# One-hot rows of two index tables stored tile by tile, and a sum of tokens with its first gather put ahead of a query product

## The chip, the cores and the metric

The kernel runs on one core of one Trainium2 chip. The metric is the device time of one execution in microseconds, lower is better. A core has a matrix engine (PE, with its weight loads listed apart as PEld), a vector engine (DVE), a scalar engine (ACT), GpSimd (POOL) and a sync engine (SP), which here issues most DMAs. Each engine works through its own instructions in order and waits on semaphores of the others.

## The reference

An attention block with sketched features feeds a mixture of experts with one expert for each token.

```python
a, b = einsum('rd,bhsd->bhsr', S1, x), einsum('rd,bhsd->bhsr', S2, x)  # phi of q and of k
phi = outer(a, b)                      # 8 x 8 = 64 features for each head and token
kv = einsum('bhsf,bhsd->bhfd', k_p, v); z = sum(k_p, axis=2)
attn = (q_p @ kv) / (q_p @ z + 1e-6)   # B=4, H=4, S=1088, D=32
x = attn.transpose(0, 2, 1, 3).reshape(4352, 128)
logits = normed(x) @ normed(expert_emb).T / tau          # 8 experts
expert_idx = argmax(logits); gate = softmax(logits)[expert_idx]
out[t] = gate[t] * (relu(x[t] @ w1[e]) @ w2[e]),  e = expert_idx[t]   # F = 1024
```

## The kernel before

The 4352 tokens are handled in two halves m = 0 and m = 1 (two batches each). A half has 17 tiles of 128 tokens (`NC`). The program has three stages that overlap. First, for each half, keys and values are summed into `kv` and `z`, and query features `qp` are made, turned and multiplied (`nd`), and `x` writes the attention rows with their router logits into `xg`. Second, a router for each half picks an expert for each token (`best`, `pick`), computes the token's place in a list sorted by expert (`place`, `take`, `split`), and a table turns places into token numbers. Third, 35 blocks of 128 sorted tokens are fetched by indirect DMA (`fetch`), turned, and run through `up` (w1, `ps_big<-xTb,wb`) and `down` (w2, `ps_acc` or `ps_ab<-w_sb,hT`) of their expert.

The table is the part that the change touches. A place is split in a block number `place_k` and a lane `place_r` (scaled so that it equals lane / 128). `mark` (lines 775 to 780) makes, for each tile t of tokens, a 128 x 128 matrix of zeros and ones, token by lane, by comparing `place_r` with `lanes`; all of them lie in one bf16 tile `row`, of which `row[:, :, t]` is tile t. `find` and `digit` (L844, L848) mark which block a token belongs to and put its token number there (`hits`). `sums` (lines 850 to 856) multiplies, on PE, `row[:, :, t]` as weights with the `hits` of tile t, and adds over the tiles in PSUM: 17 matmuls with 20 moving columns for the first table, which serves the first 10 blocks (half m = 0), and 34 with 56 columns for the second, which serves the other 25. `tokens` (L872) on DVE reduces the result to the list `dst_i` of token numbers, which POOL's gathers (`fetch`, L1043) use.

The order on each engine is written out by hand. `HEAD` and `ORDER` (lines 395 to 410) are lists of steps in program order; every step issues its instructions to whichever engines it uses, and each engine's order follows from it. The steps that matter here are, in `ORDER`: `mark 00` and `mark 01` (DVE, the 17 tiles in parts of 8 and 9), `find` (DVE), `exp0` (DVE, and on SP the load of the first w1), `qab 2 acc` (PE), `sums` (PE), `qp 1` (DVE, L458, features of query group 1), `tokens` (DVE), `z1` (DVE, L536), `trqp 1` (PE, L158, turns that group), `qp 3` (DVE), `kve` (PE), `fetch0` and `fetch 1` (POOL, blocks 0 and then 1 to 3), then `nd 1 0`, `x 1 0`, `turn 0` (PE turns block 0), `nd 1 1`, `x 1 1`, and after `up(0)` comes `nd 1 2`. The second table's steps are placed by tick and rank among the blocks (lines 711 to 716 and 1201 to 1216).

Of the kernel before, what the change touches and what calls it, by code (L numbers as in the profile page):

```python
# [12 lines left out]
BF16 = mybir.dt.bfloat16  # L13
I32 = mybir.dt.int32
U32 = mybir.dt.uint32
ALU = mybir.AluOpType
# [3 lines left out]
P = 128  # L20
# [6 lines left out]
HALF = P // 2  # L27
# [3 lines left out]
NM = B // 2  # L31
# [6 lines left out]
WIDE = SPAN + SPAN % 2  # L38
NEXT = 172
TWO_BANKS = (2, 3)  # L40
NCP = 8 + WIDE
# [24 lines left out]
def bview(t, free):  # L66

    return bass.AP(tensor=t.tensor, offset=t.offset, ap=[list(t.ap[0])] + [list(d) for d in free])
# [3 lines left out]
def kernel(  # L72
# [13 lines left out]
    nc = tc.nc  # L86
# [3 lines left out]
    consts = ctx.enter_context(tc.tile_pool(name="consts", bufs=1))  # L90
# [4 lines left out]
    def ps_small():  # L95
        return psum.tile([P, 512], F32, tag="t", bufs=2, name="ps_t")
# [57 lines left out]
    def mm(*args, **how):  # L154
        last["pe"] = nc.tensor.matmul(*args, **how)  # L155
# [62 lines left out]
    for h in range(H):  # L218
# [6 lines left out]
    top, rem, w, fits = (work.tile([2 * R, D], U32, tag=tag, bufs=2 if tag == "iota" else 1, name=name)  # L225
                         for tag, name in (("kv", "s_top"), ("iota", "s_rem"), ("parts", "s_w"), ("iota", "s_fits")))
# [39 lines left out]

    prefer = consts.tile([P, E], F32, name="prefer")
    lane = consts.tile([P, P], F32, name="lane")
    lanes = consts.tile([P, P, WIDE], BF16, name="lanes")
    digits = consts.tile([P, 2, NM * NCP], BF16, name="digits")  # L270

    before, ones = consts.tile([P, P], BF16, name="before"), consts.tile([P, P], BF16, name="ones")
# [12 lines left out]
    c_early = consts.tile([P, E + 1], F32, name="c_early")  # L285
    w_late = consts.tile([P, E], F32, name="w_late")
    place_k = consts.tile([P, NM * NCP], F32, name="place_k")
    place_r = consts.tile([P, NM * NCP], BF16, name="place_r")
    row = consts.tile([P, P, NM * NCP], BF16, name="row")

    nowhere = [consts.tile([P, 2, n], BF16, name=f"nowhere{n}") for n in (EARLY, LATE + SHARED)]

    def more_constants():
        nc.vector.memset(ones, 1.0 / P)
        nc.vector.memset(fours, 4.0 / P)
        nc.vector.memset(ones_e, 1.0)

        nc.vector.memset(less, -(P - 1) / (2.0 * P))
        nc.vector.memset(more, (QUART - 1) / (2.0 * P))

        nc.vector.memset(near, -(HALF + 1) / (2.0 * P))
        for i, rank in enumerate(RANKS):
            nc.vector.memset(order[:, i:i + 1], float(rank))
        nc.vector.memset(c_early, 0.0)
        nc.vector.memset(w_late, float(KEYS * E))
        for t in (place_k, place_r):
            nc.vector.memset(t, -1.0)
        for t, n in zip(nowhere, (EARLY, LATE)):
            nc.vector.memset(t, 0.0)
            nc.vector.memset(t[:, 0, :n], float(NOWHERE))  # L310
# [17 lines left out]
        nc.vector.tensor_scalar(last_first, lane[:, :E], -1.0, float(E - 1), op0=ALU.mult, op1=ALU.add)  # L328

    def wide_lanes():  # L330
        nc.vector.tensor_scalar_mul(lanes, bview(lane, [[1, P], [0, WIDE]]), 1.0 / P)

    def digits_of():
        tok_i = work.tile([P, 3, NM * NCP], I32, tag="iota", bufs=2, name="tok_i")
# [53 lines left out]
    acc, z_of, sums_of, ab_ps = {}, {}, {}, {}  # L388
# [15 lines left out]
nd 0 0; ld; ld; kab 3 ab; ld; x 0 0; ktr r; nd 0 1; ld; kab 2 t; kab r ab; ld; x 0 1; kb 2; trqp0r; nd 0 2; ld; kb 3; kp 1; kb r; nd 0 3; ld; x 0 2;  # L404
kv 0; ld; kp 2; x 0 3; qtr 1; kp 3; qtr 0; ld; kv 2; qab 0 t; qb 0; kp r; best 0; kv 3; qtr 3; qtr r; qp 0;
place 0; count; take 0; qtr 2; ld; kv 1; ld; kv r; trqp 0; total; split 0; qab 1 t; qab 3 ab; rest; mark 00; qb 1;
qab r ab; mark 01; find; exp0; qab 2 acc; sums; qb 2; qpT 0; qb 3; qb r; qp 1; tokens; z1; trqp 1; qp 3; kve; fetch0; fetch 1;
trqp 3; qpT 1; kz; qp 2; nd 1 0; ld; ld; qp r; others; w 1; x 1 0; qpT 3; norm 0; trqp 2; ld; turn 0; ld; nd 1 1; ld; x 1 1;
qpT 2
"""  # L410
# [317 lines left out]
    def router(m, c0, c1, g, bank):  # L728
        n = c1 - c0
        s = {}  # L730

        def best():
            mx = work.tile([P, n], F32, tag=f"mx_{n}", name="mx")
            nc.vector.reduce_max(out=mx, in_=lg[g][:, :n], axis=AX.X)
            nc.vector.tensor_sub(xg[g][:, :n, DM:DM + E], lg[g][:, :n], mx.unsqueeze(2).broadcast_to([P, n, E]))

        def pick():

            t = work.tile([P, n, E], F32, tag=f"lt_{n}", name="lt")
            mx = work.tile([P, n], F32, tag=f"mx8_{n}", name="mx8")  # L740
            nc.vector.scalar_tensor_tensor(out=t, in0=xg[g][:, :n, DM:DM + E], scalar=0.0,
                                           in1=bview(prefer, [[0, n], [1, E]]), op0=ALU.is_equal, op1=ALU.add)
            nc.vector.reduce_max(out=mx, in_=t, axis=AX.X)
            last["oh"] = nc.vector.tensor_tensor(out=oh[m, c0], in0=t, in1=mx.unsqueeze(2).broadcast_to([P, n, E]),
                                                 op=ALU.is_equal)
            with nc.allow_low_precision(reason="a count of at most SPAN is whole in bfloat16"):
                nc.vector.reduce_sum(out=total[m, c0], in_=oh[m, c0].rearrange("p j e -> p e j"), axis=AX.X)

        def place():

            hot = oh[m, c0]
            ps = s["ps"] = bank()[:, :n * E].rearrange("p (j e) -> p j e", e=E)
            mm(ps, before, hot, start=True, stop=False)
            for t in [base, less] + counts:
                mm(ps, ones, t.unsqueeze(1).broadcast_to([P, n, E]), start=False, stop=False)
            for j in range(1, n):
                mm(ps[:, j:], ones, hot[:, j - 1:j].broadcast_to([P, n - j, E]), start=False, stop=j == n - 1)
            counts.append(total[m, c0])  # L760

        def take():
            s["t"] = work.tile([P, n, E], F32, tag=f"lt_{n}", name="lt")
            nc.vector.tensor_mul(s["t"], s["ps"], oh[m, c0])

        def split():

            t0, t1 = m * NCP + c0, m * NCP + c1
            f = work.tile([P, n], F32, tag=f"mx8_{n}", name="mx8")
            nc.vector.reduce_sum(out=f, in_=s["t"], axis=AX.X)  # L770
            nc.vector.tensor_scalar(place_k[:, t0:t1], f, WHOLE, -WHOLE, op0=ALU.add, op1=ALU.add)
            nc.vector.scalar_tensor_tensor(out=place_r[:, t0:t1], in0=f, scalar=(P - 1) / (2.0 * P), in1=place_k[:, t0:t1],
                                           op0=ALU.add, op1=ALU.subtract)

        def mark(a=c0, b=c1):

            w = b - a + (b - a) % 2
            t0, t1 = m * NCP + a, m * NCP + a + w
            nc.vector.tensor_tensor(out=row[:, :, t0:t1], in0=lanes[:, :, :w],  # L779
                                    in1=bview(place_r[:, t0:t1], [[0, P], [1, w]]), op=ALU.is_equal)  # L780

        def write():
            for i in range(c0 // NK, c1 // NK):
                at = (2 * m + i) * S
                nc.sync.dma_start(rows[at:at + SK].rearrange("(p c) d -> p c d", p=P), xg[g][:, i * NK - c0:(i + 1) * NK - c0])
            if c1 == NC:
                for i in range(2):
                    at = (2 * m + i) * S + SK
                    nc.sync.dma_start(rows[at:at + HALF], xg[g][i * HALF:(i + 1) * HALF, 2 * NK - c0])
        return best, pick, place, take, split, mark, write  # L790


# [32 lines left out]
    def column(name, dt=F32, w=E):  # L825
        return consts.tile([P, w], dt, name=name)

    def table(which, m1, key):
# [3 lines left out]
        n, w = SIZES[which] + SECONDS[which], m1 * NCP  # L832
        s = {}
# [16 lines left out]
        def sums():  # L850
            s["ps"] = ps_small()[:, :2 * n]
            tiles = [m * NCP + c for m in range(m1) for c in range(NC)]
            mm(s["ps"], ones, nowhere[which].rearrange("p d n -> p (d n)"), start=True, stop=False)
            for t in tiles:
                mm(s["ps"], row[:, :, t], s["col"].rearrange("p d n w -> p w d n")[:, t].rearrange("p d n -> p (d n)"),
                                 start=False, stop=t == tiles[-1])

        def first_rows():
# [44 lines left out]
    def plan_late():  # L903


        left, upto, t = column("left"), column("upto1"), column("steps")
# [4 lines left out]
        s = {}  # L911
# [86 lines left out]
        def extra():  # L998
# [16 lines left out]
            f = column("extra_f", w=1)[0:1]  # L1015
# [4 lines left out]
            w = NM * NCP  # L1020
            hit = work.tile([P, 3, w], BF16, tag="lg0", bufs=1, name="extra_hit")
# [3 lines left out]
            ps = ps_small()[:, :2]  # L1025
            tiles = [m * NCP + c for m in range(NM) for c in range(NC)]
            mm(ps, ones, nowhere[0][:, :, 0], start=True, stop=False)
            for t in tiles:
                mm(ps, row[:, :, t], hit[:, 1:, t], start=False, stop=t == tiles[-1])
            with nc.allow_low_precision(reason="whole numbers of at most NOWHERE"):  # L1030
                nc.vector.reduce_sum(out=dst_i[2], in_=ps, axis=AX.X)
        return count, rest, shared, others, experts, number, start, extra
# [164 lines left out]
    count, rest, shared, others, experts, number, start, extra = plan_late()  # L1197
    find, high, low, sums, tokens, first_rows, halves = table(1, NM, lambda: late["key"])
# [106 lines left out]
```

## Time and profile before

| | us |
|---|---|
| runs of the kernel | 199.03, 200.95, 201.89 (median 200.95) |
| the profiled execution's own time | 199.14 |
| its span, first to last instruction | 197.2 |
| PE busy | 188.3 (95% of the span) |
| DVE busy | 87.9 (45%) |
| ACT busy | 99.1 (50%) |
| POOL busy | 107.6 (55%) |

The profile is of one execution. Its times count from the first instruction; the execution's own time is 1.94 us more than the span. A line of the timeline merges neighbouring instructions of one kind: start, time from the first one's start to the last one's end, engine, source line, operation, output <- input, and in brackets the idle time just before it with what ended it. Matmuls are pipelined, so a merged line ends about 0.2 us after the last one began. The fp32 matmuls appear as two passes each.

### The profile page before, as it was taken

The numbers are of one execution on the slowest core, as the hardware profiler recorded it, in microseconds if no ns is written. First come the engines' busy times: TensorE is split into PE (matmuls) and PEld (weight loads), VectorE is DVE, ScalarE is ACT, GpSimd is POOL, SyncE is SP. The second block draws the span as 40 slices with busy tenths as digits, with TensorE's granted clock in tenths as the row PEclk, the third lists the DMA queues.
The fourth block names the chain that finished last, engine by engine and source line by source line (L and its number), as shares of the span: only waits on it lengthen the run. The fifth ranks groups of instructions, "written<-read, shape, count | busy, mean of one in ns | idle before, by whom it ended". The sixth has DMA issues, their size and how long they took to land.

```text
span 197.2 us, 7104 instructions
## 1 busy us (share of the span) xinstructions
PE 188.3 (95%) x2667; PEld 177.8 (90%) x2667; DVE 87.9 (45%) x393; ACT 99.1 (50%) x280; POOL 107.6 (55%) x135
## 2 busy tenths in 40 slices
PE   7999899999979999999999999999999999999990
PEld 7677799788869999999999999999999999998890
DVE  6589868798378489922221221221221221222100
ACT  2675542437253456433564654654654654766430
POOL 4300054707713866565977767767767767733052
PEclk9999999999999999999999999999999999999999
DMA  5979968974799997544587686596665655540001
GB/s 139 345 203 276 237 172 221 331 232 124 201 281 330 285 338 209 188 136 149 149 263 237 158 288 201 155 281 211 161 195 182 160 200 180 150 137 12 3 20 32
DMA packets 29924, 38.32 MB, mean 194 GB/s; under 512 B 5721, under 2 KB 23394, under 8 KB 29890
## 3 DMA queue, kind: packets, MB, share of 16 engines
q1 hardware_dynamic: 27600, 33.18, 56.3%
q0 software_dynamic: 2240, 4.67, 7.6%
q8 instruction: 23, 0.38, 0.8%
q14 instruction: 11, 0.09, 0.2%
q10 hardware_dynamic: 50, 0.01, 0.0%
HBM read 33.25 MB, written 4.66 MB: 192 GB/s over the span
## 4 chain that ended last, share of the span: by engine, by line
PE 75%; DMA 12%; DVE 6%; issue 2%; ACT 2%; POOLq 1%; POOL 0%
PE ps_big L155 35%; PE ps_acc L155 14%; PE ps_ab L155 14%; DMA xs<-rows,dst_i 12%; PE ps_t L158 6%; PE ps_t L155 3%; PE ps_acc L111 1%; DVE xg L679 1%; DVE row L779 1%; PE ps_ab L158 1%; PE ps_acc L158 1%; POOLq L1300 1%; DVE qp L458 1%; PE ps_big L158 1%; ACT hT L1108 1%
## 5 line engine op out<-in xcount | busy, mean ns | idle before, releaser
L155 PE MATMUL ps_big<-xTb,wb 128*128 128x128 f32 (+2 forms) x608 | 70.6, 266 | 0.1
L155 PEld LDWEIGHTS ps_big<-xTb,wb 128*128 128x128 f32 (+1 forms) x608 | 66.7, 183 | 1.5 <-issue 0.9
L1149 POOL DMA_INDIRECT out_dram<-y,dst_i x35 | 36.4, 1041 | 42.3 <-ACT sq L1113 21.4
L1108 ACT ACTIVATE hT<-ps_big 128x1024 f32<-128x1024 f32 x35 | 35.8, 1023 | 41.3 <-issue 23.6
L1043 POOL DMA_INDIRECT xs<-rows,dst_i x35 | 36.7, 1048 | 13.0 <-issue 6.1
L155 PE MATMUL ps_acc<-w_sb,hT 128*128 (+2 forms) x288 | 35.1, 275 | 0.0
L1051 DVE COPY xTb<-ps_t 128x128 f32<-128x128 f32 x28 | 8.1, 291 | 57.3 <-issue 39.7
L155 PEld LDWEIGHTS ps_acc<-w_sb,hT 128*128 128x128 f32 (+2 forms) x288 | 33.3, 184 | 0.3 <-issue 0.2
L155 PE MATMUL ps_ab<-w_sb,hT 128*128 (+1 forms) x272 | 33.2, 275 | 0.0
L155 PEld LDWEIGHTS ps_ab<-w_sb,hT 128*128 128x128 f32 (+1 forms) x272 | 31.6, 187 | 0.1
L1114 POOL TENSOR_TENSOR norm<-norm,half_c 128x1 f32<-128x1 f32 x35 | 20.7, 595 | 5.2 <-ACT sq L1113 4.9
L1127 DVE TENSOR_SCALAR gate<-gate 128x1 f32<-128x1 f32 x35 | 5.3, 150 | 21.2 <-ACT probs L1124 19.7
L458 POOL TENSOR_TENSOR kp<-both 128x1024 f32<-128x1024 f32 (+1 forms) x4 | 7.2, 1812 | 12.5 <-ACT both L499 11.1
L155 PE MATMUL ps_big<-kz,held 128*64 128x82 f32 x256 | 10.7, 236 | 1.1 <-ACT xTb L1051 1.1
L1146 ACT ACTIVATE y<-ps_ab,gate 128x128 f32<-128x128 f32 x17 | 6.2, 367 | 10.9 <-PE ps_ab L155 7.1
L155 PEld LDWEIGHTS ps_big<-kz,held 128*64 128x64 f32 x256 | 9.5, 136 | 2.3 <-ACT hT L1108 1.3
L1113 ACT ACTIVATE sq<-xs 128x128 f32<-128x128 f32 x35 | 10.6, 302 | 1.5 <-DMA xs<-rows,dst_i 1.3
L1124 ACT ACTIVATE probs<-xs,norm 128x8 f32<-128x8 f32 x35 | 10.3, 295 | 1.3 <-DVE norm L1118 1.3
L1146 ACT ACTIVATE y<-ps_acc,gate 128x128 f32<-128x128 f32 x17 | 6.2, 366 | 9.4 <-PE ps_acc L155 7.0
L158 PE MATMUL ps_t<-ident,xs 128*128 128x128 f32 x35 | 9.8, 279 | 0.0
L425 ACT COPY qT<-ps_t 128x512 f32<-128x512 f32 (+1 forms) x10 | 5.1, 535 | 7.2 <-PE ps_t L158 7.2
L458 DVE TENSOR_TENSOR kp<-both 128x1024 f32<-128x1024 f32 (+1 forms) x6 | 6.4, 1088 | 2.9 <-ACT both L499 2.8
(254 smaller groups left out, 254.4 us busy)
## 6 DMA issues: line engine op xcount, KB each, us to landing
wb<-in_moe_w_dram SPq DMA_DIRECT2D x35, 512.0 KB
w_sb<-in_moe_w_dram SPq DMA_DIRECT2D x16, 256.0 KB
rows<-xg SPq DMA_DIRECT2D x4, 544.0 KB
q<-in_q_dram SPq DMA_DIRECT2D x6, 256.0 KB
k<-in_k_dram SPq DMA_DIRECT2D x3, 512.0 KB
held<-in_moe_w_dram SPq DMA_DIRECT2D x3, 512.0 KB
v<-in_v_dram SPq DMA_DIRECT2D x2, 512.0 KB
v<-in_v_dram SPq DMA_DIRECT2D x4, 256.0 KB
```

Source lines behind the costliest of these rows:

```text
L155: last["pe"] = nc.tensor.matmul(*args, **how)
L158: last["pe"] = nc.tensor.transpose(*args)
L458: last[tag] = engine.tensor_mul(t.rearrange("p j h (i k) -> p (j h) i k", i=R), ab[:, :, 0].unsqueeze(3).broadcast_to([P, n * H, R, R]), b ...
L1043: nc.gpsimd.indirect_dma_start(out=xs[i][:], out_offset=None, in_=rows[:2 * S if t == 0 else N + 1], in_offset=bass.IndirectOffsetOnAxis(a ...
L1051: (nc.scalar.copy if i < 2 or 4 <= i <= 8 else nc.vector.tensor_copy)(xT[i], ps[:, :P])
L1108: nc.scalar.activation(hT[i], ps, ACT.Relu)
L1113: nc.scalar.activation(sq, xs[i][:, :DM], ACT.Square, accum_out=norms[i])
L1114: nc.gpsimd.tensor_tensor(out=norms[i], in0=norms[i], in1=half_c, op=ALU.pow)
L1124: nc.scalar.activation(p, xs[i][:, DM:], ACT.Exp, scale=norms.pop(i)[:, 0:1], accum_out=gate[i])
L1127: nc.vector.tensor_scalar_add(gate[i], gate[i], PROB_EPS)
L1146: nc.scalar.activation(y, ps, ACT.Copy, scale=gate.pop(i)[:, 0:1])
L1149: d = nc.gpsimd.indirect_dma_start(out=out[:, :], out_offset=bass.IndirectOffsetOnAxis(ap=dst_i[t][:, j:j + 1], axis=0), in_=y[:], in_offs ...
```

## The change

Four edits go together. The tile `row` is stored with the tile number ahead of the lane: tile t is now `row[:, t]`, 128 neighbouring bf16 numbers, where before its 128 numbers lay 36 numbers apart. `lanes` shrinks from 128 x 10 numbers to 128. `place_r` holds every number twice, and `mark` compares two neighbouring lanes with such a pair, for 8 and 9 tiles (before 8 and 10, the odd count being padded); the memset of `place_r` that the padding called for goes. And in `ORDER`, `tokens` and `fetch0` stand ahead of `qp 1`, with `fetch 1` left where it was. The extra path at the end (L1029), which these inputs do not run, reads `row` in the new way as well.

```diff
-    lanes = consts.tile([P, P, WIDE], BF16, name="lanes")
+    lanes = consts.tile([P, P], BF16, name="lanes")
...
-    place_r = consts.tile([P, NM * NCP], BF16, name="place_r")
-    row = consts.tile([P, P, NM * NCP], BF16, name="row")
+    place_r = consts.tile([P, NM * NCP, 2], BF16, name="place_r")
+    row = consts.tile([P, NM * NCP, P], BF16, name="row")
...
-        for t in (place_k, place_r):
-            nc.vector.memset(t, -1.0)
+        nc.vector.memset(place_k, -1.0)
...
-        nc.vector.tensor_scalar_mul(lanes, bview(lane, [[1, P], [0, WIDE]]), 1.0 / P)
+        nc.vector.tensor_scalar_mul(lanes, lane, 1.0 / P)
...
-qab r ab; mark 01; find; exp0; qab 2 acc; sums; qb 2; qpT 0; qb 3; qb r; qp 1; tokens; z1; trqp 1; qp 3; kve; fetch0; fetch 1;
+qab r ab; mark 01; find; exp0; qab 2 acc; sums; qb 2; qpT 0; qb 3; qb r; tokens; fetch0; qp 1; z1; trqp 1; qp 3; kve; fetch 1;
...
-            nc.vector.scalar_tensor_tensor(out=place_r[:, t0:t1], in0=f, scalar=(P - 1) / (2.0 * P), in1=place_k[:, t0:t1],
+            nc.vector.scalar_tensor_tensor(out=place_r[:, t0:t1], in0=f.unsqueeze(2).broadcast_to([P, n, 2]),
+                                           scalar=(P - 1) / (2.0 * P),
+                                           in1=place_k[:, t0:t1].unsqueeze(2).broadcast_to([P, n, 2]),
                                            op0=ALU.add, op1=ALU.subtract)
...
-            w = b - a + (b - a) % 2
-            t0, t1 = m * NCP + a, m * NCP + a + w
-            nc.vector.tensor_tensor(out=row[:, :, t0:t1], in0=lanes[:, :, :w],
-                                    in1=bview(place_r[:, t0:t1], [[0, P], [1, w]]), op=ALU.is_equal)
+            w, t0 = b - a, m * NCP + a
+            nc.vector.tensor_tensor(out=row[:, t0:t0 + w].rearrange("p t (l d) -> p t l d", d=2),
+                                    in0=bview(lanes, [[0, w], [2, HALF], [1, 2]]),
+                                    in1=bview(place_r[:, t0:t0 + w], [[2, w], [0, HALF], [1, 2]]), op=ALU.is_equal)
...
-                mm(s["ps"], row[:, :, t], s["col"].rearrange("p d n w -> p w d n")[:, t].rearrange("p d n -> p (d n)"),
+                mm(s["ps"], row[:, t], s["col"].rearrange("p d n w -> p w d n")[:, t].rearrange("p d n -> p (d n)"),
```

On DVE, the instructions from the first table's two `mark`s on stand like this before. In brackets is the engine whose semaphore an instruction waits for; `row` is the marks' output, `hits` that of `find` and `digit`, `exp` that of `exp0`, `qp<-both` is the step `qp 1`, `dst_i` the step `tokens`, `z` the step `z1`.

```order
L779 TENSOR_TENSOR row<-lanes,place_r 128x128x8
L779 TENSOR_TENSOR row<-lanes,place_r 128x128x10
L844 TENSOR_TENSOR hits_1075<-at_1062,place_k 128x180 [waits DVE_49]
L848 TENSOR_TENSOR hits_1075<-hits_1075,digits 128x18x10 [waits DVE_49]
L848 TENSOR_TENSOR hits_1075<-hits_1075,digits 128x18x10
L818 TENSOR_REDUCE exp_f_1065<-le_1061 1x10
L819 TENSOR_SCALAR exp_210<-exp_f_1065 1x1 [waits DVE_49]
L458 TENSOR_TENSOR qp<-both 128x1024 [waits Activation_49]
L872 TENSOR_REDUCE dst_i_207<-ps_t 128x10 [waits PE_49]
L536 TENSOR_TENSOR z<-own,kv 128x256 x2
```

And like this with the change, in the same place of the same engine (source lines are one or two off, since lines were added and taken out).

```order
L779 TENSOR_TENSOR row<-lanes,place_r 128x1024
L779 TENSOR_TENSOR row<-lanes,place_r 128x1152
L845 TENSOR_TENSOR hits_1074<-at_1061,place_k 128x180 [waits DVE_49]
L849 TENSOR_TENSOR hits_1074<-hits_1074,digits 128x18x10 [waits DVE_49]
L849 TENSOR_TENSOR hits_1074<-hits_1074,digits 128x18x10
L819 TENSOR_REDUCE exp_f_1064<-le_1060 1x10
L820 TENSOR_SCALAR exp_210<-exp_f_1064 1x1 [waits DVE_49]
L873 TENSOR_REDUCE dst_i_207<-ps_t 128x10 [waits PE_49]
L457 TENSOR_TENSOR qp<-both 128x1024 [waits Activation_49]
L535 TENSOR_TENSOR z<-own,kv 128x256 x2
```

`dst_i`, which waits for PE's sums, moved ahead of `qp`, which does not; the marks' outputs became runs of 1024 and 1152 neighbouring numbers. On PE, ACT, POOL and SP every instruction stands where it stood.

The second table's marks stand on DVE between instructions of the blocks; here are the second mark and its neighbours with the change (before, the `row` line reads `128x128x10`, in the same place).

```order
L845 TENSOR_TENSOR hits_1707<-at_1608,place_k 128x1008
L849 TENSOR_TENSOR hits_1707<-hits_1707,digits 128x36x28
L779 TENSOR_TENSOR row<-lanes,place_r 128x1152
L1118 TENSOR_SCALAR norm<-norm 128x1
L1119 RECIPROCAL norm<-norm 128x1
```

Nothing moved there; only the mark's layout and its size differ.

## Rows read from the trace of the kernel before

**Rows 1.** The page's first two parts: busy time, share of the span and instructions of each engine, and the clock that PE was granted in 40 slices of the span, in tenths of full speed.

```profile
PE 188.3 (95%) x2667; PEld 177.8 (90%) x2667; DVE 87.9 (45%) x393; ACT 99.1 (50%) x280; POOL 107.6 (55%) x135
...
PEclk9999999999999999999999999999999999999999
```

**Rows 2.** Busy time by stretch of the span: start and end, length, then each engine's busy time and count, PE's granted clock, the DMA engines' busy share and GB/s.

```profile
45.10:51.80 6.70, 6.70 (x114) 5.93 (x114) 5.33 (x14) 4.14 (x12) 5.44 (x5) 1.00 0.54 145
51.80:55.70 3.90, 2.69 (x19) 2.12 (x21) 1.50 (x5) 1.51 (x3) 1.56 (x2) 1.00 1.00 286
55.70:85.70 30.00, 30.00 (x338) 29.61 (x339) 22.72 (x107) 15.76 (x53) 17.37 (x20) 1.00 0.81 256
85.70:87.80 2.10, 2.10 (x38) 2.10 (x35) 0.15 (x1) 0.37 (x1) 1.01 (x1) 1.00 0.63 215
87.80:165.70 77.90, 77.90 (x700) 77.78 (x699) 18.24 (x111) 40.97 (x125) 56.02 (x64) 1.00 0.65 196
165.70:192.40 26.70, 26.68 (x469) 24.94 (x467) 4.48 (x27) 14.46 (x36) 11.45 (x13) 1.00 0.24 75
```

**Rows 3.** Timeline of PE around the first table's sums and the step `trqp 1` behind them.

```profile
43.66 1.16 PE L155 MATMUL ps_t<-hits,row 128*128 128x20 bf16 x17
45.09 1.09 PE L158 MATMUL ps_big<-ident,qp 128*128 128x128 f32 x8 [0.27 <-DVE qp L458]
```

**Rows 4.** Timeline of DVE over the same stretch: the two marks, the end of `exp0`, `qp 1`, `tokens`, `z1`.

```profile
41.28 1.42 DVE L779 TENSOR_TENSOR row<-lanes,place_r 128x1024 bf16<-128x1024 bf16 x2
...
43.76 0.14 DVE L819 TENSOR_SCALAR exp<-exp_f 1x1 int32<-1x1 f32 x1
43.83 1.20 DVE L458 TENSOR_TENSOR qp<-both 128x1024 f32<-128x1024 f32 x1
44.97 0.16 DVE L872 TENSOR_REDUCE dst_i<-ps_t 128x10 int32<-128x20 f32 x1
45.05 0.74 DVE L536 TENSOR_TENSOR z<-own,kv 128x256 f32<-128x256 f32 x2
```

**Rows 5.** Timeline of PE and of DVE around the second table's sums.

```profile
85.72 2.22 PE L155 MATMUL ps_t<-hits,row 128*128 128x56 bf16 x34
87.78 2.03 PE L155 MATMUL ps_big<-xTb,wb 128*128 128x128 f32 x16
...
82.82 1.19 DVE L848 TENSOR_TENSOR hits<-hits,digits 128x1008 bf16<-128x1008 bf16 x1
...
87.98 0.20 DVE L872 TENSOR_REDUCE dst_i<-ps_t 128x20 int32<-128x40 f32 x1 [2.13 <-PE ps_t L155]
```

**Rows 6.** PE's weight loads of bf16, grouped by what is loaded: partitions x numbers, count, busy us, mean ns of one. `ones` and `before` are constant tiles whose 128 numbers are neighbours.

```profile
L155 PEld LDWEIGHTS <-row 128*128 128x128 bf16 x51 | 3.2, 167 | 0.0
...
L155 PEld LDWEIGHTS <-ones 128*128 128x128 bf16 x48 | 1.9, 97 | 0.7 <-issue 0.6
...
L155 PEld LDWEIGHTS <-before 128*128 128x128 bf16 x3 | 0.3, 99 | 0.0
```

**Rows 7.** Timeline of weight loads in the second half's `place` steps, whose matmuls have 72 moving columns or fewer.

```profile
64.45 0.34 PEld L155 LDWEIGHTS <-ones 128*128 128x128 bf16 x10
...
68.46 0.52 PEld L155 LDWEIGHTS <-ones 128*128 128x128 bf16 x16
```

**Rows 8.** DVE's instructions grouped by line and shape: count, busy us, mean ns of one, idle time before them.

```profile
L848 DVE TENSOR_TENSOR hits<-hits,digits 128x1008 bf16<-128x1008 bf16 x2 | 2.4, 1200 | 0.0
...
L779 DVE TENSOR_TENSOR row<-lanes,place_r 128x1280 bf16<-128x1280 bf16 x2 | 1.6, 818 | 0.0
...
L779 DVE TENSOR_TENSOR row<-lanes,place_r 128x1024 bf16<-128x1024 bf16 x2 | 1.4, 695 | 0.0
...
L848 DVE TENSOR_TENSOR hits<-hits,digits 128x180 bf16<-128x180 bf16 x2 | 0.6, 342 | 0.0
```

**Rows 9.** Timeline of POOL, ACT and PE, one after the other: block 0's gather, the first reader of its rows, and PE from its turn on (`nd 1 1` at 50.43, `up(0)` at 51.78, `nd 1 2` at 55.63, and `up(2)` at 62.65).

```profile
45.42 1.45 POOL L1043 DMA_INDIRECT xs<-rows,dst_i  x1 [5.61 <-DVE dst_i L872]
...
49.01 0.31 ACT L1113 ACTIVATE sq<-xs 128x128 f32<-128x128 f32 x1 [0.18 <-DMA xs<-rows,dst_i]
...
50.23 0.27 PE L158 MATMUL ps_t<-ident,xs 128*128 128x128 f32 x1
50.43 1.36 PE L155 MATMUL ps_big<-kz,held 128*64 128x82 f32 x32
51.78 2.63 PE L155 MATMUL ps_big<-xTb,wb 128*128 128x128 f32 x16
...
55.63 1.36 PE L155 MATMUL ps_big<-kz,held 128*64 128x82 f32 x32 [1.10 <-ACT xTb L1051]
...
62.65 1.96 PE L155 MATMUL ps_big<-xTb,wb 128*128 128x128 f32 x16
```

**Rows 10.** Timeline of DVE: `lanes` and the next long idle time behind it; then the last instruction of `x 1 0`, and the first of `x 1 1` and the last that reads the PSUM product of `nd 1 1`.

```profile
22.81 0.82 DVE L331 TENSOR_SCALAR lanes<-lane 128x1280 bf16<-128x1280 f32 x1
...
26.31 1.23 DVE L458 TENSOR_TENSOR kp<-both 128x1024 f32<-128x1024 f32 x1 [1.47 <-ACT both L499]
...
50.83 0.38 DVE L684 TENSOR_REDUCE lg<-parts 128x32 f32<-128x128 f32 x1
54.10 0.18 DVE L677 TENSOR_SCALAR rc<-ps_big 128x16 f32<-128x16 f32 x1 [2.88 <-remote]
...
55.20 0.28 DVE L683 TENSOR_TENSOR parts<-ps_big,rc 128x128 f32<-128x128 f32 x1
```

More of the change, by code (lines that the diff above doesn't have):

```diff
@@ L1028, in extra @@
             for t in tiles:
-                mm(ps, row[:, :, t], hit[:, 1:, t], start=False, stop=t == tiles[-1])
+                mm(ps, row[:, t], hit[:, 1:, t], start=False, stop=t == tiles[-1])
             with nc.allow_low_precision(reason="whole numbers of at most NOWHERE"):
```

## The prediction

> **What bounds the kernel now.** I read the page first: PE is busy for 95% of the span and its granted clock is full in all 40 slices, that is the 2.4 GHz level throughout [rows 1]. So the question for every edit is whether PE gets the time back or loses it. A busy share over the whole span hides where PE waits, so next I read the busy times by stretch. From 55.70 on PE has no idle time that matters: 30.00 of 30.00, 2.10 of 2.10, 77.90 of 77.90 and 26.68 of 26.70 us [rows 2]. Whatever is taken out of PE's work there shortens the program by as much, and nothing else does. From 45.10 to 51.80 PE is full too (6.70 of 6.70), so a delay that enters at 45.10 travels to 51.80 unchanged. Only 51.80 to 55.70 has slack, 2.69 busy of 3.90. Then the timeline, for the places that the change touches: the first table's sums, 17 matmuls from 43.66 to 44.82, and `trqp 1` behind them, for which PE waits 0.27 us until DVE's `qp 1` is done [rows 3, 4]; and the second table's 34 matmuls, which hold PE from 85.72 to 87.78 in the full stretch [rows 5].
>
> **The second table's sums, the gain.** 34 matmuls in 87.78 - 85.72 = 2.06 us are 60.6 ns each [rows 5]. With 56 moving columns they should not need that: matmuls with `ones` as weights and 72 columns or fewer follow each other at (0.34 - 0.097) / 9 = 27 and (0.52 - 0.097) / 15 = 28 ns [rows 6, 7]. The visible difference is the weight load: 167 ns in the mean for `row`, whose 128 numbers lie 36 numbers (72 bytes) apart, and 97 to 99 for tiles of the same size and type whose numbers are neighbours [rows 6]. With the change `row[:, t]` is such a tile. The bounds are no gain (60.6 stay) and 27 ns; I take 28, since in shape and type the new load is the one in those rows, and `before`, which is loaded once at a time and not again and again like `ones`, also takes 99. Gain: 34 x (60.6 - 28) = 1.11 us, all of it in a stretch where PE never waits. The marks and digits that these sums need are early enough: the last digit ends at 82.82 + 1.19 = 84.01, 1.7 us ahead of 85.72 [rows 5].
>
> The Trainium skill, "TensorE: Matmul & The Clock Gate", section on weight-path perf modes, says that the fast weight load is on for 128 weights of a type other than fp32 and reads its chunks packed or strided, within a step of some thousand elements. By that rule alone old and new load would be equally fast and the 1.11 us would not come; 167 against 97 ns in this trace says that the step does cost, and I go by the rows. What the rule would make of the time is the third rival below.
>
> **The first table's sums and the new order, the loss.** The same 32 ns on 17 matmuls end the sums 0.54 us sooner, at 44.28 instead of 44.82 [rows 3]. Before, this would have been worth nothing: PE's next work waits for `qp 1`, which DVE began at 43.83 while the sums ran [rows 4]. With the change `tokens` stands first on DVE and waits for the sums. In the second table it starts 0.04 us after the last sum ends (85.72 + 2.22 = 87.94, then 87.98) [rows 5], so here at 44.32, and the next instruction starts 0.08 later as now (44.97, 45.05) [rows 4]: `qp 1` starts at 44.40, not 43.83. PE starts `trqp 1` 1.26 us after `qp 1` starts (43.83, 45.09), so at 45.66: a delay of 0.57 us. Behind `tokens` on DVE wait `qp 1`, `z1` and the later products, moved by 0.5 us or less since `tokens` no longer stands between them; PE, moved by 0.57, does not wait for them anew.
>
> Two smaller terms come ahead of it. The marks go from 1024 and 1280 numbers to 1024 and 1152; by their own slope, (818 - 695) / 256 = 0.48 ns a number, that is 0.06 us less [rows 8]. `place_r` is written twice over, 17 numbers more at (1200 - 342) / 828 = 1.04 ns: 0.02 us more [rows 8]. Sums, `tokens` and `qp 1` start 0.04 sooner, so the delay is 0.53 us.
>
> What the order is to buy is an earlier first gather. It starts on POOL 0.45 us after `tokens` (44.97, 45.42) [rows 4, 9], so at 44.73, 0.7 us sooner. Its rows are first read at 49.01 on ACT, and PE turns the block at 50.23, in its own order and without waiting [rows 9]. Block 0's rows are thus over a microsecond early already and the gain there is nothing; the cover is PE's own queue. Gathers 1 to 3 follow sooner by as much and are not waited for either. `lanes` shrinks to a tenth (0.82 us now), but DVE then idles 1.47 us until ACT hands it `kp`'s input [rows 10]: nothing on the path. The memset that goes lies at the very start, far ahead of any of this; I cost it at nothing too.
>
> **Does the delay reach the end?** It travels to 51.80. There stands a stall whose cause the trace does not name: `up(0)` takes 2.63 us where `up(2)` takes 1.96, and `nd 1 2` waits 1.10 us [rows 9], because its PSUM bank is held by `x 1 1`, which DVE starts at 54.10 after 2.88 us of idle time put down to "remote", though `nd 1 1` was done at 51.79 [rows 9, 10]; the DMA engines are busy all through this stretch [rows 2]. If the end of that wait is tied to DVE's and PE's progress, the 0.53 passes through; if it is tied to something that the change does not move, the slack swallows it. I take the first, since the instructions on both sides of the wait move together, and keep zero as the other bound.
>
> **Sum.** -1.11 + 0.53 = -0.58 us against the profiled execution's own 199.14: 198.56. That execution is a quick one: the mean of it and the three runs shown is 200.25, 1.11 above it. For the median of the changed kernel's runs I add that 1.11: **199.7 us**.
>
> **Rivals.**
> 1. The stall swallows the delay: only the 1.11 us remain, 198.03 on the profiled basis, 199.1 in the median. For it: the wait is long and its releaser is none of the moved engines. It could also vanish altogether (0.67 + 1.10 more): 196.8, or 197.9 in the median.
> 2. The other side: the marks run at one number a cycle. The new `place_r` operand is a pair read 64 times over, a pattern that no row shows. `L848`, also bf16 on both sides, takes 342 ns for 180 numbers and 1200 for 1008 [rows 8]; at that rate the marks take 1.22 and 1.35, 2.57 us against 1.42 now [rows 4], and everything behind them, `trqp 1` too, is late by 0.57 + 0.02 + 1.15 = 1.74 us. Sum: -1.11 + 1.74 = +0.63, or 199.8 and 200.9 in the median. It decides the sign once the two marks together take 0.6 us longer than forecast. Against it: all three operands still step by one number innermost, as in the marks of now, which run at 0.48 ns a number. The second table's marks would be 1.0 us longer and fit into their 1.7.
> 3. The loads do not get faster: the sums still end at about 44.78, `tokens` starts at 44.82, `qp 1` at 44.90, and `trqp 1` is 1.07 us late with nothing gained later: 200.2, or 201.3 in the median. Against it the 97 to 99 ns of rows 6.
>
> On rival 2, the Trainium skill's "Vector Engine (DVE) Microarchitecture Reference", section on measured stream behaviour, says that a port runs at full rate only in runs of two or more neighbouring 4-byte words, and gives 1.73 instead of 1.054 ns where one source hops at every element. A pair of `place_r` is one such word; if reading it again counts as a hop, an estimate from that page is 17 x 64 x 0.68 ns = 0.74 us more for the two marks and a sum near +0.2. No row here shows such a pattern.
>
> **Chances.** Forecast as it stands 0.50; rival 1 0.20 (0.05 of it the stall gone); rival 2 0.15; rival 3 0.10; something not seen 0.05. All medians lie between 197.9 and 201.3, and the runs shown scatter by 2.9 us; the range that leaves 2 in 10 out is **197.8 to 201.6**. A measurement of this kernel can tell about 2%, 4 us, from no change, and no case comes near that: faster 0.04, same 0.93, slower 0.03.
>
> **What would show it.** Weight loads of `row` near 97 ns; 34 sums in about 1 us; marks near 0.70 and 0.76 us; `tokens` right behind the sums and PE idle 1.3 us ahead of `trqp 1`; `up` blocks from the second table on about a microsecond earlier relative to `up(0)`. Marks above 1 us, or loads that stay at 160 ns, would make the forecast wrong, and so would a different length of the stall ahead of `nd 1 2`.

## The result and the profile after

The changed kernel takes **201.09 us** in the median of 20 runs (199.18 to 204.10), the kernel before 199.38 on the same occasion (20 runs, 198.01 to 202.71); in the means it is 201.23 against 199.74. The ratio is 1.0061 with a 95% interval of 1.0035 to 1.0087: slower by 0.4 to 0.9%, where 0.3% faster was forecast. The time lies inside the forecast range; the sign does not. The ratio leaves out runs over 1.5% above the fastest of their kernel; since the cause found below makes just such runs, the experiments are also compared by the means of all their runs.

The profiled execution took 199.18 us with a span of 197.1, against 199.14 and 197.2 before. It is one of the quickest of the 20: it shows what the edits did, and not yet why the median went up. First the page, PE's busy time and granted clock [rows 1]:

```profile
span 197.1 us, 7103 instructions
PE 186.5 (95%) x2667; PEld 175.8 (89%) x2667; DVE 87.5 (44%) x392; ACT 99.0 (50%) x280; POOL 107.1 (54%) x135
PEclk9999999999999999999999999999999999999999
```

PE does 1.8 us less work (188.3 before) in a span as long as before: the work that was saved has become idle time. The weight loads of bf16 by what is loaded, and the marks on DVE (count, busy us, mean ns) [rows 6, 8], are as forecast:

```profile
L155 PEld LDWEIGHTS <-ones 128*128 128x128 bf16 x48 | 1.9, 97 | 0.4 <-issue 0.3
...
L155 PEld LDWEIGHTS <-row 128*128 128x128 bf16 x51 | 1.5, 96 | 0.0
...
L779 DVE TENSOR_TENSOR row<-lanes,place_r 128x1152 bf16<-128x1152 bf16 x2 | 1.5, 751 | 0.0
L779 DVE TENSOR_TENSOR row<-lanes,place_r 128x1024 bf16<-128x1024 bf16 x2 | 1.4, 678 | 0.0
```

Timeline of PE around the second table's sums [rows 5]: 0.97 us from their start to the next `up`, where it was 2.06.

```profile
86.07 1.04 PE L155 MATMUL ps_t<-hits,row 128*128 128x56 bf16 x34
87.04 2.02 PE L155 MATMUL ps_big<-xTb,wb 128*128 128x128 f32 x16
```

Timeline of DVE and of PE around the first table's sums [rows 3, 4]; line 873 is `tokens`, line 457 the products, the first of them `qp 1`:

```profile
43.23 0.14 DVE L820 TENSOR_SCALAR exp<-exp_f 1x1 int32<-1x1 f32 x1
43.97 0.18 DVE L873 TENSOR_REDUCE dst_i<-ps_t 128x10 int32<-128x20 f32 x1 [0.60 <-PE ps_t L155]
44.06 1.21 DVE L457 TENSOR_TENSOR qp<-both 128x1024 f32<-128x1024 f32 x1
45.20 0.75 DVE L535 TENSOR_TENSOR z<-own,kv 128x256 f32<-128x256 f32 x2
```

```profile
43.00 0.39 PE L155 MATMUL ps_acc<-Sblk,qT 128*64 128x64 f32 x5 [0.38 <-issue]
...
43.36 0.57 PE L155 MATMUL ps_t<-hits,row 128*128 128x20 bf16 x17
45.33 1.09 PE L158 MATMUL ps_big<-ident,qp 128*128 128x128 f32 x8 [1.40 <-DVE qp L457]
...
47.20 0.66 PE L158 MATMUL ps_acc<-ident,qp 128*128 128x128 f32 x4
...
49.36 1.36 PE L155 MATMUL ps_big<-kz,held 128*64 128x82 f32 x32 [1.07 <-issue]
...
51.82 1.36 PE L155 MATMUL ps_big<-kz,held 128*64 128x82 f32 x32
```

DVE is free at 43.37 and waits 0.60 us for the sums, only then come `tokens` and `qp 1`, and PE waits 1.40 us ahead of `trqp 1`, where it waited 0.27. Counted from the start of the sums, `trqp 1` begins after 45.33 - 43.36 = 1.97 us, where it was after 45.09 - 43.66 = 1.43: the change delays it by 0.54 us in place. PE stands still three times within 7 us: 0.38, 1.40 and 1.07 us. Busy time by stretch [rows 2] (PE, its weight loads, DVE, ACT, POOL, granted clock, DMA) shows what this does later:

```profile
45.10:51.80 6.70, 5.40 (x81) 4.68 (x81) 4.44 (x12) 3.07 (x7) 4.84 (x5) 1.00 0.43 118
51.80:55.70 3.90, 3.90 (x64) 3.62 (x65) 3.06 (x10) 1.75 (x4) 0.99 (x1) 1.00 0.79 191
```

The stall of 51.8 to 55.7 is gone; the 1.07 us of "issue" ahead of `nd 1 0` (the row at 49.36) are new. DVE was half a microsecond ahead of the profile before already at the end of `exp0` (43.23, 43.76), so the two executions can't be subtracted row by row here. The page of this execution shows the full clock all through; what it can't show is that most of the others did not have it. The mean granted clock of the 20 runs goes from 0.970 to 1.000, and 13 of them lie under 0.99 (of the 20 runs of the kernel before on that occasion only the times are known). That is where the theories part.

### The profile page after: what moved, and what is told of

Its sections match the earlier page's. It is cut to its first block, busy times and chain, and to the rows that moved or that the text cites. A ratio compares the mean times of both kernels' runs of the same rounds, so it can differ in the third digit from the quotient of the medians.

```text
span 197.1 us, 7103 instructions
## 1 busy us (share of the span) xinstructions
PE 186.5 (95%) x2667; PEld 175.8 (89%) x2667; DVE 87.5 (44%) x392; ACT 99.0 (50%) x280; POOL 107.1 (54%) x135
## 4 chain that ended last, share of the span: by engine, by line
PE 72%; DMA 12%; DVE 6%; issue 5%; POOL 2%; ACT 1%; POOLq 1%
PE ps_big L155 32%; PE ps_ab L155 14%; PE ps_acc L155 14%; DMA xs<-rows,dst_i 12%; PE ps_t L158 6%; PE ps_t L155 3%; PE ps_acc L111 1%; DVE xg L678 1%; PE ps_big L158 1%; POOL xs L1044 1%; POOL norm L1115 1%; DVE lg L683 1%; PE ps_ab L158 1%; PE ps_acc L158 1%; POOLq L1301 1%
## 5 line engine op out<-in xcount | busy, mean ns | idle before, releaser
L1044 POOL DMA_INDIRECT xs<-rows,dst_i x35 | 36.2, 1034 | 11.7 <-issue 6.3
```

Of the source, the lines that this page charges most:

```text
L1044: nc.gpsimd.indirect_dma_start(out=xs[i][:], out_offset=None, in_=rows[:2 * S if t == 0 else N + 1], in_offset=bass.IndirectOffsetOnAxis(a ...
```

## Experiments

**Theory A**: the longer idle time of PE ahead of `trqp 1` lowers the granted clock in many executions. **B**: the order costs its plain delay, the clock has no part. **C**: the layout itself costs. **D**, added later: it is the earlier gather, not the wait. Each run had runs of the kernel before beside it on its chip: 23 on the first chip (layout alone, order alone, nine transposes, changed kernel), 29 on the second (wait alone, order filled, nine again, four) and 29 on the third (the rest), with means of 198.31, 198.55 and 198.81 us and 2, 5 and 6 of them under a mean clock of 0.99. "Low" below is the number of runs under 0.99; differences are those of the means of all runs with 95% intervals (1.96 standard errors; for six runs that is about a quarter too narrow, which changes no conclusion). A fall of the clock is a stretch at the lower of its two levels; what one looks like is shown below.

**The layout alone**, twice:

```diff
-qab r ab; mark 01; find; exp0; qab 2 acc; sums; qb 2; qpT 0; qb 3; qb r; tokens; fetch0; qp 1; z1; trqp 1; qp 3; kve; fetch 1;
+qab r ab; mark 01; find; exp0; qab 2 acc; sums; qb 2; qpT 0; qb 3; qb r; qp 1; tokens; z1; trqp 1; qp 3; kve; fetch0; fetch 1;
```

> The new layout of the row one-hots with the old order (tokens behind qp 1, first gather behind kve). Theory A, the clock: the order's longer idle time of PE ahead of trqp 1 (1.40 us in the changed kernel, 0.27 before) makes the granted clock fall in many executions, and the layout by itself only gains; here PE waits some 0.8 us there, so the ratio to the kernel before is 0.993 to 0.998, with a mean granted clock nearer to that of the kernel before than to the changed kernel's 0.97 to 1.00. Theory B, the plain delay: the order costs its 0.5 us at qp 1 and further waits behind it, the clock has no part in it: 1.1 us gained, ratio 0.994, clocks no matter. Theory C, the layout itself costs (shorter sums leave PE idle, or the marks disturb something): ratio 1.003 or more.

> The new layout with the old order, again, for more runs. Theory A: mean time 0.6 to 1.1 us below the kernel before, granted clocks of 0.99 to 1.00 as in the kernel before. Theory B: 1.1 us below.

Measured: ratio 0.9968 (0.9933 to 1.0003), difference -0.74 +-0.76 us, low 0 of 12; then 0.9999 (0.9955 to 1.0044), -0.42 +-1.09, low 1 of 12, less of a gain than expected. Together -0.58 +-0.67. In the two profiles PE waits 0.31 and 0.57 us ahead of `trqp 1`, not 0.8. Theory C falls: the layout does not cost. That it gains is likely, that it gains its whole 1.1 us is not shown.

**The order alone**, the kernel before with the opposite edit of that line:

> The kernel before with the new order alone, old layout. Sums end at 44.82 as before, tokens and qp 1 follow, so trqp 1 is about 1.07 us late and PE waits 1.3 us ahead of it. Theory A (clock): 1.1 us of delay and granted clocks below 1 in many runs, ratio 1.008 to 1.02. Theory B (plain delay): ratio 1.003 to 1.006, granted clocks as in the kernel before. Theory C (layout costs): ratio 1.000 to 1.005, less than the changed kernel's loss.

Measured: ratio 1.0148 (1.0084 to 1.0211), +2.67 +-1.8 us, low 4 of 6. More than the delay, and with lower clocks: A, not B. Its profiled execution kept the full clock, and has the wait in it (timeline of PE; the second row is `nd 1 1`):

```profile
45.27 1.09 PE L158 MATMUL ps_big<-ident,qp 128*128 128x128 f32 x8 [1.40 <-DVE qp L458]
...
50.58 1.36 PE L155 MATMUL ps_big<-kz,held 128*64 128x82 f32 x32
```

**The changed kernel again**, on two chips:

> The changed kernel again, on the same chip as the other three, so that its runs and granted clocks stand beside theirs. All theories: ratio 1.0035 to 1.009 to the kernel before, granted clocks of 0.97 to 1.00.

> The changed kernel a third time, beside the other three. Theory A: granted clocks below 0.99 in 4 to 8 of 10 runs, mean time 0.7 to 1.8 us above the kernel before; the runs at 0.995 and more 0.3 to 0.9 us below those of the kernel before at such clocks. Theory B: no difference between the two groups of runs.

Measured: ratio 0.9964 (0.9913 to 1.0014) on the first chip and 1.0150 (1.0084 to 1.0216) on the third, where 1.0035 to 1.009 was expected: one below, one above. By the means of all runs it is +1.19 +-1.4 us with 8 of 13 low, and +1.75 +-1.1 with 4 of 6 low. On the first chip the 8 low runs take 200.8 us in the mean, the other 5 197.5, 0.7 less than the 21 runs of the kernel before that are not low (198.1), as theory A has it. On the third chip that expectation fails: the two runs that are not low take 199.7 and 200.1, against 198.2 in the mean of the 23 runs of the kernel before that are not low. On the first chip the profile caught a low run. PE's clock by slice, the timeline of PE, then PE's busy time and granted clock in stretches of 2 us:

```profile
PEclk9999969999589999999999999999999999999998
```

```profile
47.06 0.39 PE L155 MATMUL ps_acc<-Sblk,qT 128*64 128x64 f32 x5 [1.35 <-issue]
...
47.42 0.57 PE L155 MATMUL ps_t<-hits,row 128*128 128x20 bf16 x17
49.40 1.38 PE L158 MATMUL ps_big<-ident,qp 128*128 128x128 f32 x8 [1.40 <-DVE qp L457]
...
52.19 1.11 PE L158 MATMUL ps_acc<-ident,qp 128*128 128x128 f32 x4
...
57.78 0.43 PE L155 MATMUL ps_big<-kz,held 128*64 128x82 f32 x6
```

```profile
46.00:48.00 2.00, 0.93 (x23) 1.00 0.20 57
48.00:50.00 2.00, 0.60 (x6) 1.00 0.80 219
50.00:52.00 2.00, 2.00 (x27) 0.52 0.29 86
52.00:54.00 2.00, 2.00 (x14) 0.50 0.27 67
54.00:56.00 2.00, 2.00 (x29) 0.50 0.16 37
56.00:58.00 2.00, 2.00 (x23) 0.78 0.33 33
```

This is how a fall of the clock is read: PE stands still for most of 46 to 50 us, in two waits of 1.35 and 1.40; after it has gone on with `trqp 1`, the granted clock is 0.50, the 1.2 GHz level, and PE is "busy" without a gap because every matmul takes longer (four transposes 1.11 us, 0.66 in the profile after). From `trqp 1` to `nd 1 1` it takes 57.78 - 49.40 = 8.38 us; in the run of the order alone, at the full clock, 50.58 - 45.27 = 5.31. **A fall here costs 3.07 us in place.** Two more profiles below have a fall there, with 8.30 us (wait alone) and 8.42 (four transposes) for the same stretch; the profiles with the full clock and no stop inside it have 5.30 to 5.38 (5.34 before). The profile after is at the full clock too but has its 1.07 us of "issue" inside, so it takes 51.82 - 45.33 = 6.49, and against that a fall costs 1.9. The 6 in the sixth slice is a second fall (granted clock 0.54 and 0.60 in 26 to 28 and 28 to 30 us), behind a stop of 2.48 us that ends at 25.74, ahead of all that the change touches.

**The gap filled with work that nothing needs**: nine transposes of the identity into `trqp 1`'s own PSUM bank, ahead of it, twice; and four.

```diff
+    FILL = 9
...
+            for _ in range(FILL if (m, c0) == (1, 4) else 0):
+                tp(s["ps"][0][:, :P], ident, ident)
             for p in range(2):
                 for j in range(n):
```

> The changed kernel plus nine transposes of the identity, written into trqp 1's own PSUM bank just ahead of it, so that PE is busy for about 1.2 us of its 1.40 us of idle time there; nothing else moves. Theory A (clock): granted clock back to 1.0 in nearly all runs, 0.5 to 2 us less than the changed kernel, ratio to the kernel before 0.995 to 1.000. Theory B and C: same time as the changed kernel, ratio 1.004 to 1.008, clocks below 1 as often as there.

> The changed kernel with the nine filling transposes, again, for more runs. Theory A: granted clocks of 0.99 to 1.00, mean time 0.3 to 1.0 us below the kernel before (1.11 of gain less the delay of 0.5). Theory B and D: as the changed kernel, 0.5 to 2 us above.

> The changed kernel with four filling transposes instead of nine: PE still waits about 0.85 us ahead of trqp 1. Theory A, if the clock answers to the length of PE's idle time: between the changed kernel and the filled one, clocks below 0.99 in some runs but fewer than with no filling, mean time 0.5 us below to 1.0 above the kernel before. Theory B and D: as the changed kernel.

Measured with nine: -0.78 +-1.4 us, low 0 of 6 (no ratio), then ratio 0.9899 (0.9820 to 0.9979), -0.03 +-1.5, low 1 of 6, less of a gain than the 0.3 to 1.0 expected. With four: ratio 0.9973 (0.9922 to 1.0024), +1.0 +-1.35, low 3 of 12, at the upper end of what was expected. PE in the first run with nine:

```profile
43.32 0.57 PE L155 MATMUL ps_t<-hits,row 128*128 128x20 bf16 x17
43.74 1.18 PE L158 MATMUL ps_big<-ident 128*128 128x128 f32 x9
45.29 1.09 PE L158 MATMUL ps_big<-ident,qp 128*128 128x128 f32 x8 [0.37 <-DVE qp L458]
```

`trqp 1` starts at the same time (45.29, 45.33 in the profile after), PE has more to do, and low runs go from 12 of 19 to 1 of 12, with 3 of 12 in between for the half dose. B and D have no answer to this.

**The order alone, filled**: both edits above on the kernel before.

> The kernel before with the new order (old layout) and the nine filling transposes ahead of trqp 1. Theory A: granted clocks of 0.99 to 1.00 in nearly all runs, mean time 0 to 1.2 us above the kernel before, against 2.7 us above it for the new order without the filling. Theory B and D: clocks of 0.97 to 0.99 as often as with the new order alone, 2 to 3 us above.

Measured: ratio 1.0018 (0.9976 to 1.0060), +0.28 +-0.87 us, low 1 of 12, as A has it. What the order costs beyond its delay goes with the idle time.

**The wait alone**: old layout, old order, but `qp 1` is computed twice.

```diff
             s["qp"] = features(s["ab"], s["b"], n, "qp", nc.gpsimd if by_pool else nc.vector)
+            if (m, c0) == (1, 4):
+                nc.vector.tensor_mul(s["qp"].rearrange("p j h (i k) -> p (j h) i k", i=R),
+                                     s["ab"][:, :, 0].unsqueeze(3).broadcast_to([P, n * H, R, R]),
+                                     s["b"].unsqueeze(2).broadcast_to([P, n * H, R, R]))
```

> The kernel before, old layout and old order, with the product of qp 1 computed twice into the same tile. DVE gives qp 1 to PE 1.1 to 1.2 us later, and PE waits about 1.4 us ahead of trqp 1 as it does in the changed kernel; tokens and the first gather are not moved ahead. Theory A (the idle time lowers the clock): mean granted clock 0.97 to 0.99 in about half of the runs or more, mean time 1.5 to 3.5 us above the kernel before. Theory B (plain delay): 1.1 us above it, clocks as in the kernel before (0.99 to 1.00). Theory D (it is the earlier gather's traffic that disturbs, not the wait): clocks and times as in theory B, or less.

Measured: ratio 1.0094 (1.0044 to 1.0143), +2.66 +-0.94 us, low 8 of 12. Neither `tokens` nor the gather is earlier here, so D falls: a late `qp 1` is enough. The profile caught a fall (timeline of PE, the last row `nd 1 1`, then the stretches). PE waits 0.80 us for `qp 1` there and not 1.4, because a stop of 0.93 us ahead of it had already made the sums late:

```profile
45.50 0.39 PE L155 MATMUL ps_acc<-Sblk,qT 128*64 128x64 f32 x5 [0.93 <-issue]
...
47.80 1.97 PE L158 MATMUL ps_big<-ident,qp 128*128 128x128 f32 x8 [0.80 <-DVE qp L602]
...
56.10 1.36 PE L155 MATMUL ps_big<-kz,held 128*64 128x82 f32 x32
```

```profile
44.00:46.00 2.00, 1.07 (x28) 1.00 0.58 165
46.00:48.00 2.00, 1.21 (x19) 0.88 0.50 90
48.00:50.00 2.00, 2.00 (x12) 0.50 0.46 182
```

**The gap filled with work that is needed**: `z1` on DVE ahead of `tokens` or `qp 1`, `kve` on PE ahead of `trqp 1`; once with the new order of `tokens`, once with the old one.

```diff
-qab r ab; mark 01; find; exp0; qab 2 acc; sums; qb 2; qpT 0; qb 3; qb r; tokens; fetch0; qp 1; z1; trqp 1; qp 3; kve; fetch 1;
+qab r ab; mark 01; find; exp0; qab 2 acc; sums; qb 2; qpT 0; qb 3; qb r; z1; tokens; fetch0; qp 1; kve; trqp 1; qp 3; fetch 1;
```

```diff
-qab r ab; mark 01; find; exp0; qab 2 acc; sums; qb 2; qpT 0; qb 3; qb r; tokens; fetch0; qp 1; z1; trqp 1; qp 3; kve; fetch 1;
+qab r ab; mark 01; find; exp0; qab 2 acc; sums; qb 2; qpT 0; qb 3; qb r; z1; qp 1; tokens; kve; trqp 1; qp 3; fetch0; fetch 1;
```

> The changed kernel with z1 ahead of tokens and kve ahead of trqp 1: DVE makes z1 while it waits for the sums, and PE has kve's 0.84 us in its 1.40 us of idle time, so that no work is added. Theory A: PE waits 0.5 to 0.7 us ahead of trqp 1, the clock stays at 0.99 to 1.00 in most runs, and PE is 0.8 us further than in the changed kernel: mean time 0.5 to 1.5 us below the kernel before. Theory B (clock without a part): 0.8 us less than the changed kernel's mean, so 0.4 us above to 0.4 below the kernel before.

> The new layout with tokens behind qp 1 as before, z1 ahead of qp 1 and kve ahead of trqp 1. qp 1 starts 0.7 us later than with the layout alone, and PE has kve meanwhile. Theory A: PE waits 0.2 to 0.5 us, clocks of 0.99 to 1.00, mean time 0.6 to 1.4 us below the kernel before, like the layout alone or 0.3 less. Theory B: the same time, as the clock has no part in either.

Measured: the first, ratio 0.9995 (0.9953 to 1.0037), -0.79 +-0.94 us, low 3 of 12; the second, ratio 1.0033 (0.9978 to 1.0088), +0.24 +-1.0, low 4 of 12. The first repairs the changed kernel without adding work (-0.79 against +1.75 beside it), and the fall that its profile has lies elsewhere, at 24 to 32 us (granted clock 0.83 and 0.75 in two stretches of 4 us), ahead of all that is changed here. Its PE timeline, `kve` and then `trqp 1`:

```profile
46.60 0.50 PE L155 MATMUL ps_t<-by_head,kv 128*64 128x80 f32 x8
...
48.07 1.09 PE L158 MATMUL ps_big<-ident,qp 128*128 128x128 f32 x8 [0.56 <-DVE qp L457]
```

The second was expected 0.6 to 1.4 us below the kernel before and is not: in its profile PE waits 0.64 us a step later, ahead of `trqp 3`. `kve` no longer stands between the two steps, and `qp 3` on DVE itself waits 0.49 us for ACT (timeline of DVE, then of PE):

```profile
47.98 1.23 DVE L457 TENSOR_TENSOR qp<-ps_ab,qb 128x1024 f32<-128x1024 f32 x1 [0.49 <-ACT both L452]
...
49.26 0.66 PE L158 MATMUL ps_acc<-ident,qp 128*128 128x128 f32 x4 [0.64 <-DVE qp L457]
```

From the sums to `nd 1 1` PE takes 52.70 - 46.18 = 6.52 us in this profile, as long as in the first of the layout alone (51.46 - 44.94): nothing was gained on it. No version is faster than the kernel before beyond doubt: the one ratio with its whole interval below 1 (0.9899, nine transposes) has a difference of the means of -0.03 +-1.5 beside it. The layout alone and the first of these two have the lowest means.

## Why the prediction was wrong

**The gain was right.** Row loads 96 ns (97 forecast), marks 678 and 751 ns (0.70 and 0.76 us forecast), 34 sums in 0.97 us: 2.06 - 0.97 = 1.09 against 1.11. So rivals 2 (slow marks) and 3 (slow loads) did not happen. Both places where the prediction read the Trainium skill as speaking against the change come out by the rows: 96 ns for a packed load and 167 for a strided one, against "TensorE: Matmul & The Clock Gate", section on weight-path perf modes; and no extra cost for a pair that is read again and again, where the prediction's own estimate from "Vector Engine (DVE) Microarchitecture Reference", section on measured stream behaviour, had 0.74 us. The earlier gather bought nothing, as forecast: POOL starts it at 44.45 (45.42 before), and PE turns the block at 51.61 (50.23) [rows 9].

**The mechanism of the loss was right.** `tokens` came right behind the sums (43.36 + 0.57 = 43.93, then 43.97), `qp 1` 0.09 us after it, `trqp 1` 1.27 us after that (1.26 forecast), and PE waited 1.40 us where 1.3 was named as the sign to look for. The delay of `trqp 1`, 0.54 us counted from the start of the sums, agrees with the 0.53 in the prediction's sum.

**The step that failed** is the price of that wait. The prediction says of `trqp 1` "a delay of 0.57 us" and lets it pass on "unchanged"; it takes the clock as "the 2.4 GHz level throughout" from one execution and never asks whether the edit could change it. But the same edit that delays `trqp 1` by half a microsecond lengthens PE's idle time by 1.13 us (0.27 to 1.40), for the sums also end sooner; and that idle time has a price of its own in many executions:

- kernels with the 1.40 us wait or one like it (changed, order alone, wait alone): low clock in 13 of 20, 12 of 19, 4 of 6 and 8 of 12 runs;
- kernels with that gap short or filled (before, layout alone, nine transposes with either layout): 13 of 81, 1 of 24, 2 of 24;
- in between, four transposes and the two with `kve` moved: 3 of 12, 3 of 12 and 4 of 12.

The mark of 0.99 is a choice; the one fall in the profile of the wait alone makes a mean of 0.983. With 0.985 in its place the first line reads 11 of 20, 8 of 19, 4 of 6 and 8 of 12, the second 7 of 81, 1 of 24 and 1 of 24. Where the falls of the runs without a profile lie is not known. The ratios alone, too, put the kernels with the long wait (1.0061, 1.0148, 1.0094, 1.0150) above the rest (0.9899 to 1.0033), but for the 0.9964 of the changed kernel on the first chip.

The size is an estimate. If every low run has one such fall, it costs 3.07 us in 13 of 20 instead of 13 of 81 runs: (0.65 - 0.16) x 3.07 = 1.50. With the forecast -0.58 this makes +0.9, where the changed kernel showed +1.71 in the median and +1.49 in the mean at first, and +1.19 and +1.75 in the means later. By whole runs the price is smaller: low runs take 2.3 us more than the other runs of the same kernel on the same chip, in the mean over all kernels, which makes 1.1 and a sum of +0.5. For the wait alone, the expected delay of 1.1 to 1.2 and (8/12 - 5/29) x 3.07 = 1.52 make 2.6 to 2.7, measured 2.66 +-0.94; that it comes so close is luck with such an interval. None of the rivals had this: all moved work and waits at a fixed clock.

**The stall** of 51.8 to 55.7, which rival 1 had swallow the delay or vanish, was an accident of one execution: the profile of the order alone, with the old layout and a later `trqp 1`, has `nd 1 1` followed by 16 matmuls of `up(0)` and `nd 1 2` without idle time, and in none of the 13 other profiles does PE wait there. A stall without a named releaser should not have carried a rival with 0.20.

**The basis** was off too: +1.11 from the profiled execution to the median rested on four runs. With 20 runs the median before is 199.38, so the forecast of 199.7 was nearer to 201.09 than its own steps earned: on that basis they give 198.8, and the range would end at 200.7. That the time fell inside the range is luck.

What stays open: why the layout alone shows -0.58 +-0.67 and not -1.1 in the whole time, though its profiles show the 1.1 us in place (the 34 sums take 0.96 us in both). The interval does not exclude -1.1, and the spread of the executions ahead of the first `up` (in the 14 profiles, `up(0)` starts between 51.78 and 59.14) may hide it. And in the changed kernel +0.5 to +0.9 is reckoned and +1.2 to +1.75 measured: the 7 of the first 20 runs that are not low take 200.1 us in the mean, more than the mean before, and the two on the third chip are slower too, so something beside the falls may cost there.

The Trainium skill, "TensorE: Matmul & The Clock Gate", section on HAM oscillation, tells of a kernel whose clock falls again and again because PE waits for transfers between its tiles. The runs here agree that PE's waits bring the clock down, with waits for another engine in place of transfers. Otherwise than there, the changed kernel falls in one execution and not in the next: low clock in 12 of 19.

## What to carry to other kernels

Price a delay on TensorE twice: as time that passes through, and as idle time that may cost the clock behind it; the second can be several times the first, and the profile of a lucky execution does not show it. So look at the granted clock of every run, not of the profiled one, and where PE must wait, put work that is ready ahead of the wait (here `kve`, 3 of 12 low) or fill the gap (2 of 24); a test with useless work in the gap tells such a cost from a plain delay, given some ten runs of it, since a fall is a matter of chance.

## What was not expected of the hardware

The waits that bring the clock down are short. In the run with four transposes PE stood still for 0.56 us ("issue") and 0.92 us (`qp 1`), with 1.4 us of matmuls between, and still fell (timeline of PE, the last row `nd 1 1`, then PE's busy time and granted clock by stretch):

```profile
42.32 0.39 PE L155 MATMUL ps_acc<-Sblk,qT 128*64 128x64 f32 x5 [0.56 <-issue]
...
44.66 1.59 PE L158 MATMUL ps_big<-ident,qp 128*128 128x128 f32 x8 [0.92 <-DVE qp L458]
...
53.08 1.36 PE L155 MATMUL ps_big<-kz,held 128*64 128x82 f32 x32
```

```profile
42.00:44.00 2.00, 1.42 (x27) 1.00 0.33 93
44.00:46.00 2.00, 1.34 (x8) 0.78 0.58 223
46.00:48.00 2.00, 2.00 (x28) 0.50 0.42 109
```

The wait for `qp 1` alone does not decide it: three profiles with 1.40 us there kept the full clock (after, order alone, and the changed kernel on the third chip).

The other part of the idle time is not the change's at all. In twelve of the fourteen profiles PE stops ahead of the same five matmuls (`Sblk`, `x5` above), for 0.20 to 1.35 us and for nothing that the profile names ("issue"). In the low run of the changed kernel PE stops at 45.71 and goes on at 47.06, and a packet of instructions was moved just ahead of that (DMA by queue, 44.40 to 45.50 us: packets, MB, share of 16 engines):

```profile
q1 hardware_dynamic: 479, 0.24, 74.2%
q8 instruction: 1, 0.02, 5.7%
```

while a data queue held most of the DMA engines' time. That PE waits there for its instructions is a guess, and was not tested. The traces bear it out further: in all twelve profiles PE goes on 2.3 to 2.7 us after such a packet of 0.02 MB begins to move, whether it has stood for 0.20 us or for 1.35.

This stop may also be what makes a fall a matter of chance. The clock fell at `trqp 1` in the three profiles whose stop was 1.35, 0.93 and 0.56 us, with 1.40, 0.80 and 0.92 us of wait for `qp 1` behind it. It stayed full where the wait was 1.40 and the stop 0.38, 0.20 or none, and where the stop was 0.80, 0.93 or 1.08 and the wait 0.31, 0.37 or none. These are nine executions and no test of it: no run changed the stop alone.
